# Retention followed by a squared-ReLU network: the first matrix product of ten groups in Strassen's form, with a table of priorities

## The chip, the cores and the metric

The kernel runs on one core of a Trainium2 chip. Its time is the device time of one execution in microseconds (us), as the median of several runs. A core has a matrix engine (TensorE; PE in the profile, with its weight loads as PEld), three engines for element-wise work (VectorE or DVE, ScalarE or ACT, GpSimd or POOL), an engine that here only issues transfers (SyncE or SP), and 16 DMA engines.

## The reference

Two stages. The first is a retention layer, attention without softmax: 8 batches, 8 heads, 576 positions, 64 numbers a head. The second takes its output, laid out as 4608 tokens of 512 numbers, through two matrix products with a squared ReLU between them.

```python
q, k, v: (8, 8, 576, 64) float32
scores = (1 / sqrt(64)) * q @ k^T
gamma[h] = 1 - 2 ** (-5 - h)
D[h, i, j] = gamma[h] ** (i - j) if i >= j else 0
a = (scores * D) @ v
x = a.transpose(0, 2, 1, 3).reshape(4608, 512)
h = x @ w_in                  # 512 x 2048
g = relu(h) ** 2
out = g @ w_out               # 2048 x 512, float32 result
```

## The kernel before

Matrix operands are float16, sums in PSUM and results float32. The tokens are cut into 36 **units** of 128: for each batch four chunks of 128 positions ("full" units) and, for the last 64 positions of two batches together, one "tail" unit. Two units make a **group** of 256 tokens; there are 18. Groups 0 to 3 are batches 0 and 1, groups 4 to 7 batches 2 and 3, group 8 the first two tail units, groups 9 to 12 and 13 to 16 the other four batches, group 17 the last two tail units.

What happens to a unit from 8 on: three loads (k, q, v; q as four transfers) are issued on SP's queue in `add_load` (L319, L316, for tails L322). GpSimd casts k and q to float16 into one tile `kq` (L394, L405) and multiplies v by a decay (L410). SP issues a DMA transpose of `kq` to `kqT` (L420). Units 0 to 7 come in pairs with wider loads and are transposed on TensorE (L461, tile psT).

What happens to a group: TensorE makes the scores (tile psc), the new states (psS) and the outputs (psO), all from small 64x64 matmuls recorded under L381. VectorE masks the scores (rT, L713), updates the states (Rm, stmp, and the decay to R, L487) and scales the outputs to `xT` (L772), which is x transposed: 128 partitions x 4 parts of the 512 numbers x 256 tokens. Scores and states of the next group are computed beside the outputs of this one.

Then the network, in `add_ff`. **First product**: 16 blocks of 128 of the 2048 columns; each is four matmuls of N=256 (one for each part of x; L896), two blocks to a PSUM tile `ph`. ScalarE takes the ReLU of a tile into `rl` (L904) and squares it into `gT` (L914); one tile in eight is squared on VectorE (L916). **Second product**, in `add_strassen`: for groups 1 to 17 it is already in Strassen's form (Winograd's variant). The product of 256 tokens x 2048 by 2048 x 512 is cut into 2x2 blocks; seven products of blocks (56 matmuls of N=256, L993, tile po) take the place of eight. For that VectorE makes four sums of blocks of g (`gS`, L966); four sums of w_out (`wT`, L848) were made once. ScalarE copies partial results out of PSUM (L1006, L1067), VectorE adds them into the output tile `o` (L1016), and SP stores it (L865, L870).

Engines and SP's queue each work strictly in order. The order is not written by hand: every piece of work is a task of class `Schedule` with an engine, a priority key, a planned duration, the tasks that it needs and the buffers that it takes. `emit` plays the tasks through in planned time; an engine that is free takes the ready task with the lowest key whose buffers are free, and instructions are emitted in that order. Keys before are formulas of the group number. The planner also slows VectorE's two-input float16 work (`soft` tasks) while GpSimd runs a long task. Buffers are counted in its dictionary: 5 for loads of each of k, q and v, 7 for `kq`, 7 for cast v, 6 for `kqT`, 3 for x, 4 for o, 8 banks of PSUM.

Of the kernel before, what the change touches and what calls it, by code (L numbers as in the profile page):

```python
# [9 lines left out]
FP32 = mybir.dt.float32  # L10
FP16 = mybir.dt.float16
ACTF = mybir.ActivationFunctionType
ALU = mybir.AluOpType


class Schedule:
# [9 lines left out]
    def add(self, eng, key, dur, fn, deps=(), acq=(), after=None, lag=0.0, soft=False):  # L26
        t = dict(soft=soft, eng=eng, key=key, dur=dur, fn=fn, acq=acq, n=len(self.tasks), users=[], free=[], lag=lag,
                 left=len(deps), ready=0.0, lat=self.LAT[eng] if after is None else after)
        for d in deps:
            d["users"].append(t)  # L30
        self.tasks.append(t)
        return t
# [11 lines left out]
    def emit(self):  # L44
        ready = {e: [] for e in self.LAT}
# [24 lines left out]
        while True:  # L70
            for e in ready:
                if busy[e]:
                    continue
                held = []
                while ready[e]:
                    item = heapq.heappop(ready[e])
                    t = item[2]
                    if all(self.count[r] >= t["acq"].count(r) for r in t["acq"]):
# [14 lines left out]
                    held.append(item)  # L93
                for item in held:
                    heapq.heappush(ready[e], item)
# [35 lines left out]
def kernel(  # L131
# [38 lines left out]
    ld = ctx.enter_context(tc.tile_pool(name="ld", bufs=5))  # L170
    stage = ctx.enter_context(tc.tile_pool(name="stage", bufs=4))
    cast = ctx.enter_context(tc.tile_pool(name="cast", bufs=7))
    work = ctx.enter_context(tc.tile_pool(name="work", bufs=4))
    o_pool = ctx.enter_context(tc.tile_pool(name="o", bufs=4))
    x_pool = ctx.enter_context(tc.tile_pool(name="x", bufs=3))
    st_pool = ctx.enter_context(tc.tile_pool(name="st", bufs=1))
    g_pool = ctx.enter_context(tc.tile_pool(name="g", bufs=3))
    u_pool = ctx.enter_context(tc.tile_pool(name="u", bufs=2))
    r_pool = ctx.enter_context(tc.tile_pool(name="r", bufs=3))
    ps_ff = ctx.enter_context(tc.tile_pool(name="ps_ff", bufs=8, space=bass.MemoryType.PSUM))  # L180
# [7 lines left out]
    wT = [const.tile([P, NF // 2, DM // 2], FP16, name=f"wT{i}") for i in range(4)]  # L188
    junk = wT[3][:, 0:2].rearrange("p f m -> p (f m)")
# [62 lines left out]
    for hp in range(NP):  # L252
# [19 lines left out]
    PAIRED = 8  # L272
    FIRST = ["k0", "q0", "v0", "k2", "q2", "v2", "w0", "w1", "w2", "w3", "w4", "w5", "w6", "w7", "k4", "q4", "v4", "k6", "q6", "v6"]
    sched = Schedule(dict(ff=8, prS=1, prO=1, g=3, ld=5, wst=4, kq=7, v16=7, rT=2, x=3, rl=3, o=4, p1=2, u2=2, u4=2,
                          R=5, Rm=2, kqT=6))
# [10 lines left out]
    def warm():  # L286
        if not warm_ps:
            warm_ps.append(ps_ff.tile([P, 512], FP32, name="warm", tag="ff"))
        nc.tensor.matmul(warm_ps[0], lhsT=junk[:, 0:P], rhs=junk, start=True, stop=True)  # L289
# [36 lines left out]
    def add_load_pair(name, u):  # L326
        n = "kqv".index(name)

        def fn():
            if name != "q":  # L330
                tile_of["stage", u] = stage.tile([P, 2, H, 2 * D], FP32, name="pair", tag="wst")
# [12 lines left out]
        loaded[name, u] = loaded[name, u + 1] = dma_task(0, 2.9 if not loaded else 1.41 if name == "q" else 1.81, fn, acq=("wst",) if name != "q" else (),  # L344
# [44 lines left out]
    def add_unit(u, base):  # L389
# [28 lines left out]
        def fx2():  # L418
            t = tile_of["kqT", u] = work.tile([P, 2 * NP, P], FP16, name="kqT", tag="kqT", bufs=6)
            nc.sync.dma_start_transpose(out=t, in_=tile_of["kq", u].rearrange("p x n -> p (x n)"))  # L420
        T["kqT", u] = [add("SP", -1, 2.60, fx2, deps=[ck, cq], acq=("kqT",), after=3.0, lag=LAG_T)]

    def add_unit_pair(u, base):
# [29 lines left out]
        sched.free("wst", xs["k"] + xs["q"])  # L453
        sched.free("wst", xs["v"])
        T["kqT", u], T["kqT", u + 1] = [], []
        for i, name in enumerate("kq"):
# [9 lines left out]
            for s in range(2):  # L466
                on_act = i == 0 or s == 0 or u > 0

                def fe(i=i, s=s, on_act=on_act):
                    if i == 0:  # L470
                        tile_of["kqT", u + s] = work.tile([P, 2 * NP, P], FP16, name="kqT", tag="kqT", bufs=6)
# [11 lines left out]
        T["kvx", u] = xs["k"] + xs["v"]  # L483

    def decay(out_, in_, n=2):
        shape = "p (s n d) -> p s n d"
        nc.vector.tensor_tensor(  # L487
# [6 lines left out]
    def add_ret_pair(g):  # L494
# [44 lines left out]
        def fr2(s):  # L539
            def f():  # L540
                if s == 0:
                    tile_of["R", g] = st_pool.tile([P, 2, NP * D], FP16, name="R", tag="R", bufs=5)
# [69 lines left out]
    def base_of(g):  # L612
        return (units_of(g)[0] - len(groups[g])) * L - EARLY
# [108 lines left out]
    def after_sums(g, t, key, res):  # L722
# [17 lines left out]
        def fr2():  # L740
            r = tile_of["R", g] = st_pool.tile([P, 2, NP * D], FP16, name="R", tag="R", bufs=5)
            decay(flat(r), flat(tile_of["tmp", g]))
# [4 lines left out]
        r2 = add("DVE", key + 0.3, 0.62, fr2, deps=[r1], acq=("R",), soft=True)  # L747
# [125 lines left out]
    T["ff2"] = []  # L873

# [3 lines left out]
    def add_ff(g):  # L878
        us = groups[g]
        n = len(us)  # L880
        base = min(us) * L

# [6 lines left out]
        for fb in range(NF // nf):  # L889
# [12 lines left out]
            def fr(fb=fb):  # L902
                t = tile_of["rl", g, fb] = r_pool.tile([P, nf, n * P], FP16, name="rl", tag="rl")
                nc.scalar.activation(out=t, in_=tile_of["ph", g, fb], func=ACTF.Relu)  # L904
# [3 lines left out]
            def fg(fb=fb, on_act=on_act):  # L908
                if fb == 0:
                    tile_of["g", g] = g_pool.tile([P, NF, n * P], FP16, name="gT", tag="gT")  # L910
                t = tile_of["g", g][:, nf * fb:nf * (fb + 1), :]
                rl = tile_of["rl", g, fb]
                if on_act:
                    nc.scalar.activation(out=t, in_=rl, func=ACTF.Square)  # L914
                else:
                    nc.vector.tensor_tensor(out=t, in0=rl, in1=rl, op=ALU.mult)  # L916
            r = add("ACT", place(4 * fb + 4) - HURRY * (g == 1 and fb == 7), 0.6, fr, deps=[f1[-1]], acq=("rl",))
            sched.free("ff", [r])
            sq.append(add("ACT" if on_act else "DVE", place(4 * fb + 6) - HURRY * (g == 1 and not on_act), 0.63 if on_act else 0.43, fg, deps=[r] + sq[:1],
                          acq=() if fb else ("g",), soft=not on_act))  # L920
            sched.free("rl", [sq[-1]])
        sched.free("x", [f1[-1]])
        base2 = base + NF * n
        if STRASSEN <= g:
            add_strassen(g, us, base2, sq)
# [26 lines left out]
    def add_strassen(g, us, base, sq):  # L952
# [7 lines left out]
        def add_sum(k, key, parts, in0, in1, op, deps, start=()):  # L960
# [171 lines left out]
```

## Time and profile before

| | |
|---|---|
| time, median of 3 runs (lowest to highest) | 289.2 us (288.98 to 289.39) |
| span of the profiled execution | 287.0 us |
| median less span | 2.2 us |
| mean granted TensorE clock | 0.998 |
| idle GpSimd time that ended with a landed k, q or v (units from 8 on) | 40.9, 32.3 and 24.8 us |
| DMA queue of SP | 114560 packets, 44.84 MB |

The span goes from the first to the last instruction of one profiled execution. The profile gives no time of its own for that execution, so the 2.2 us are what the median of the runs has over its span. A line of a group of instructions names source line, engine, operation, output and inputs, then the busy time, the mean of one in ns, and the idle time of the engine ahead of them with what ended it. A timeline line has start and duration in us and, in brackets, the idle time before. Durations of matmuls overlap, so their pace is read from the distance of their starts.

### The profile page before, as it was taken

How to read it: one execution, taken by the hardware profiler on the slowest of the kernel's cores; microseconds unless marked ns; L12 is line 12 of the kernel's file. 1: busy time of each engine (PE TensorE's matmuls, PEld its weight loads, DVE VectorE, ACT ScalarE, POOL GpSimd, SP SyncE). 2: the span in 40 equal slices, each digit the busy share in tenths (PEclk: the TensorE clock that was granted, in tenths of full speed). 3: DMA queues.
4: the chain of work that ended last, by engine and by line, in shares of the span. 5: the costliest groups of instructions: out<-in, count | busy, mean ns of one | idle time of the engine just before them, and what ended most of it. 6: DMA issues, size and time to landing. Idle time of an engine off the chain costs nothing.

```text
span 287.0 us, 10144 instructions
## 1 busy us (share of the span) xinstructions
PE 280.1 (98%) x4346; PEld 235.8 (82%) x4346; DVE 179.0 (62%) x340; ACT 189.1 (66%) x365; POOL 85.1 (30%) x123
## 2 busy tenths in 40 slices
PE   8899999999999999999999999999999999999994
PEld 3578768888888888888888888888888888888883
DVE  3783588666967557638376585867575567264632
ACT  5659984678476857759486767674857486728830
POOL 6550045333614342433424243342525000000000
PEclk9999999999999999999999999999999999999999
DMA  6999999979998897989999998979999220101004
GB/s 204 291 207 207 267 304 239 170 213 189 216 209 169 223 220 184 201 210 206 194 197 197 181 202 188 217 179 229 177 233 166 92 78 2 73 25 53 0 8 141
DMA packets 119149, 49.95 MB, mean 174 GB/s; under 512 B 94784, under 2 KB 113728, under 8 KB 119104
## 3 DMA queue, kind: packets, MB, share of 16 engines
q1 hardware_dynamic: 114560, 44.84, 69.4%
q0 software_dynamic: 4224, 4.19, 8.8%
q8 instruction: 34, 0.56, 0.8%
q10 hardware_dynamic: 320, 0.26, 0.4%
q14 instruction: 11, 0.09, 0.1%
HBM read 36.70 MB, written 9.44 MB: 161 GB/s over the span
## 4 chain that ended last, share of the span: by engine, by line
PE 94%; POOL 2%; issue 2%; DVE 0%; POOLq 0%; DVEq 0%
PE ph L896 44%; PE po L993 37%; PE psO L381 5%; PE po L936 2%; PE psS L381 2%; PE psc L381 2%; PE warm L289 1%; PE psT L461 1%; POOL mask L249 1%; POOL vx L439 0%; POOL w_in L355 0%; DVE o L1016 0%; POOL mask_full L241 0%; POOL mask_tail L241 0%; DVE p L1045 0%
## 5 line engine op out<-in xcount | busy, mean ns | idle before, releaser
L896 PE MATMUL ph<-xT,w_in 128*128 128x256 f16 x1152 | 136.9, 273 | 0.0
L896 PEld LDWEIGHTS <-w_in 128*128 128x128 f16 x1152 | 111.3, 98 | 14.2
L904 ACT ACTIVATE rl<-ph 128x512 f16<-128x512 f32 x144 | 84.3, 587 | 46.2 <-PE ph L896 44.7
L914 ACT ACTIVATE gT<-rl 128x512 f16<-128x512 f16 x118 | 74.4, 630 | 3.5
L993 PEld LDWEIGHTS <-gS 128*128 128x128 f16 x544 | 51.8, 98 | 6.6
L993 PE MATMUL po<-wT,gS 128*128 128x256 f16 x408 | 54.8, 273 | 0.0
L966 DVE TENSOR_TENSOR gS<-gT,gS 128x512 f16<-128x512 f16 (+1 forms) x51 | 31.1, 610 | 20.7 <-ACT gT L914 20.1
L993 PEld LDWEIGHTS <-gT 128*128 128x128 f16 x408 | 39.8, 98 | 4.9
L993 PE MATMUL po<-w_out,gT 128*128 128x256 f16 x272 | 36.7, 273 | 0.0
L410 POOL TENSOR_TENSOR v<-v,vdec_full 128x512 f16<-128x512 f32 x24 | 25.6, 1068 | 24.6 <-DMA v<-in_v_dram 22.5
L394 POOL CAST kq<-k 128x512 f16<-128x512 f32 x28 | 20.5, 733 | 41.7 <-DMA k<-in_k_dram 40.9
L966 DVE TENSOR_TENSOR gS<-gT 128x1024 f16<-128x1024 f16 x34 | 27.6, 813 | 6.4 <-ACT gT L914 6.3
L1006 ACT COPY u<-po 128x256 f32<-128x256 f32 x34 | 12.6, 369 | 25.1 <-PE po L993 25.0
L405 POOL CAST kq<-q 128x512 f16<-128x512 f32 x24 | 14.8, 618 | 32.5 <-DMA q<-in_q_dram 32.3
L1016 DVE TENSOR_TENSOR o<-po,u 128x256 f32<-128x256 f32 x33 | 13.9, 421 | 15.6 <-PE po L993 8.6
L772 DVE TENSOR_TENSOR xT<-psO,gam_full 128x512 f16<-128x512 f32 x28 | 18.0, 685 | 7.6 <-PE psO L381 7.4
L916 DVE TENSOR_TENSOR gT<-rl 128x512 f16<-128x512 f16 x26 | 11.6, 448 | 16.3 <-ACT rl L904 16.1
L713 DVE TENSOR_TENSOR rT<-psc,mask_full 128x512 f16<-128x512 f32 x24 | 15.5, 682 | 5.3 <-PE psc L381 5.2
L993 PE MATMUL po<-w_out,gS 128*128 128x256 f16 x136 | 17.8, 273 | 0.0
L993 PE MATMUL po<-wT,gT 128*128 128x256 f16 x136 | 17.6, 273 | 0.0
L1016 DVE TENSOR_TENSOR o<-po,p 128x256 f32<-128x256 f32 x18 | 7.6, 422 | 13.7 <-ACT u L1006 8.9
L487 DVE TENSOR_TENSOR R<-stmp,dec 128x512 f16<-128x512 f32 (+1 forms) x18 | 12.5, 694 | 0.5
(80 smaller groups left out, 219.3 us busy)
## 6 DMA issues: line engine op xcount, KB each, us to landing
out_dram<-o SPq DMA_DIRECT2D x32, 256.0 KB, 2.6
k<-in_k_dram SPq DMA_DIRECT2D x24, 256.0 KB, 4.5
q<-in_q_dram SPq DMA_DIRECT2D x96, 64.0 KB, 3.5
v<-in_v_dram SPq DMA_DIRECT2D x24, 256.0 KB, 3.9
pair<-in_k_dram SPq DMA_DIRECT2D x4, 512.0 KB, 7.1
pair<-in_q_dram SPq DMA_DIRECT2D x8, 256.0 KB, 5.9
pair<-in_v_dram SPq DMA_DIRECT2D x4, 512.0 KB, 5.5
w_in<-in_moe_w_in_dram POOLq DMA_DIRECT2D x4, 512.0 KB, 8.3
```

Source lines behind the costliest of these rows:

```text
L381: t = nc.tensor.matmul(out_, lhsT=lhsT, rhs=rhs, start=start, stop=True, skip_group_check=True, tile_position=(64 * row, 64 * col))
L394: op(out=out_.rearrange("p (n b a d) -> p n b a d", n=2, b=2, a=2), in_=in_.rearrange("p (a n b) d -> p n b a d", n=2, a=2))
L405: nc.gpsimd.tensor_copy(out=tile_of["kq", u][:, 1].rearrange("p (t a d) -> p a t d", t=4, a=2), in_=tile_of["q32", u].rearrange("p (a t) d ...
L410: nc.gpsimd.tensor_tensor(out=t, in0=tile_of["v32", u], in1=vdec[kind].rearrange("p (h o) -> p h o", o=1).to_broadcast([P, H, D]), op=ALU. ...
L713: tile_of["masking", g] = nc.vector.tensor_tensor(out=tile_of["rT", g][:, :, a], in0=tile_of["psc", g][a].rearrange("p (s n i) -> p s n i" ...
L772: nc.vector.tensor_tensor(out=tile_of["x", g].rearrange("p n (s e i) -> p e (n s) i", s=n, e=2)[:, c], in0=y.rearrange("p (o t r) -> p o r ...
L896: nc.tensor.matmul(tile_of["ph", g, fb][:, j, :], lhsT=w_in16[:, m, fi * P:(fi + 1) * P], rhs=tile_of["x", g][:, m, :], start=(m == 0), st ...
L904: nc.scalar.activation(out=t, in_=tile_of["ph", g, fb], func=ACTF.Relu)
L914: nc.scalar.activation(out=t, in_=rl, func=ACTF.Square)
L966: nc.vector.tensor_tensor(out=tile_of["S", g][:, k, sl], in0=in0(sl), in1=in1(sl), op=op)
L993: nc.tensor.matmul(tile_of["pb", g, bank], lhsT=left(i), rhs=right[:, i, :], start=(start and i == 0), stop=(i == HF - 1), skip_group_chec ...
L1016: nc.vector.tensor_tensor(out=o_tile(u)[:, half * HM:(half + 1) * HM], in0=bank(x), in1=tile_of[name, g], op=ALU.add)
```

## The change

Groups 5, 7 and 9 to 16 take the new function `add_ff1s` for the first product. x (512 numbers x 256 tokens) and w_in are cut into 2x2 blocks: 256 numbers by 128 tokens of x, 1024 columns by 256 numbers of w_in. Seven products follow for each half (j = 0, 1) of 512 columns: each is 8 matmuls of N=128 into a PSUM tile of 4 x 128. Four sums of x are made on GpSimd (three into a new tile `xS`, of which there is one; one in place in `xT`), four sums of w_in (`wS`, in eight VectorE instructions) once, into the tiles that had held the loads of units 0 and 4. Three partial results of each half are copied out of PSUM by ScalarE (p1q, u2q, u4q). Of the four blocks of a half, one gets its ReLU on ScalarE; three are made by a VectorE instruction that adds a PSUM tile and a copy and floors the sum at zero, straight into `gT`. ScalarE then squares in place, two blocks in one instruction.

Around it: in the other groups the ReLU goes straight into `gT` and is squared there (`rl` is gone). The decay of the states (R) of the groups from 4 on moves from VectorE to GpSimd. Buffers: loads 5 to 3, `kq` 7 to 6, cast v 7 to 6, o 4 to 3, wide loads and `gS` 4 to 3 with two fixed tiles beside them. The keys of nearly all of 1869 tasks come from a table (`PLACES`), and a task may not take a buffer that a task with a lower key on the same engine is waiting for.

```diff
+RESERVE = True
+PLACES = """
...
+""".split()
...
     def emit(self):
+        assert len(PLACES) == len(self.tasks)
+        for t, x in zip(self.tasks, PLACES):
+            if x != "-":
+                t["key"] = int(x)
...
-                    if all(self.count[r] >= t["acq"].count(r) for r in t["acq"]):
+                    if (t["inside"] or not kept.intersection(t["acq"])) and all(self.count[r] >= t["acq"].count(r) for r in t["acq"]):
...
+                    if RESERVE and t["key"] < 10 ** 5:
+                        kept.update(r for r in t["acq"] if self.count[r] < t["acq"].count(r))
...
+    H1, H2 = 2, 1
+    UF, OB, P1Q, WST = 2, 3, 2, 3
+    LD, KQ, V16, SB, G, UQ, KT, RB = 3, 6, 6, 0, 3, 2, 6, 5
...
+    FSET = (5, 7, 9, 10, 11, 12, 13, 14, 15, 16)
...
+    T_ENG = "POOL"
+    R_ENG = "POOL"
+    S4_ENG = "DVE"
...
-        r2 = add("DVE", key + 0.3, 0.62, fr2, deps=[r1], acq=("R",), soft=True)
+        r2 = add(R_ENG, key + 0.3, 0.62 if R_ENG == "DVE" else 1.07, fr2, deps=[r1], acq=("R",), soft=R_ENG == "DVE")
...
+    HK = NP // 2
+    wA = {(i, j): w_in16[:, HK * j:HK * j + HK, DFF // 2 * i:DFF // 2 * i + DFF // 2] for i in range(2) for j in range(2)}
...
+        s1 = add_wS(0, wA[1, 0], wA[1, 1], ALU.add, [])
+        s2 = add_wS(1, wS[0], wA[0, 0], ALU.subtract, [s1])
+        s3 = add_wS(2, wA[0, 0], wA[1, 0], ALU.subtract, [])
+        s4 = add_wS(3, wA[0, 1], wS[1], ALU.subtract, [s2])
...
+    def add_ff1s(g):
+
+        base = 2 * g * L - F1OFF
+        xs = [T["x", u] for u in groups[g]]
+        X = lambda i, s: (lambda: tile_of["x", g][:, HK * i:HK * i + HK, s * P:(s + 1) * P])
+        B11, B21, B12, B22 = X(0, 0), X(1, 0), X(0, 1), X(1, 1)
+        T1, T2, T4 = ((lambda i=i: tile_of["xs", g][:, HK * i:HK * i + HK]) for i in range(3))
+        T3 = B12
+        t = []
+        for i, (out_, in0, in1) in enumerate(((T1, B12, B11), (T3, B22, B12), (T2, B22, T1), (T4, B21, T2))):
+            def f(i=i, out_=out_, in0=in0, in1=in1):
+                if i == 0:
+                    tile_of["xs", g] = x_pool.tile([P, 3 * HK, P], FP16, name="xS", tag="xS", bufs=1)
+                (nc.vector if T_ENG == "DVE" else nc.gpsimd).tensor_tensor(out=out_(), in0=in0(), in1=in1(), op=ALU.subtract)
+            t.append(add(T_ENG, base - TKEY + i, 0.25 if T_ENG == "DVE" else 0.55, f, deps=xs + t, acq=() if i else ("xs",), soft=T_ENG == "DVE"))
...
+                for e in range(4):
+                    fi = 4 * j + e
+                    for m in range(HK):
+                        nc.tensor.matmul(out_[:, e], lhsT=left[:, m, fi * P:(fi + 1) * P], rhs=right()[:, m],
+                                         start=fresh and e == 0 and m == 0, stop=m == HK - 1, skip_group_check=True)
...
+        def relu_sum(s, h, j, x, name, key, deps, acq=()):
+            def f():
+                new_g()
+                nc.vector._custom_dve(TENSOR_ADD_SAT, out=g_at(s, h, j), in0=bank(j, x),
+                                      in1=tile_of[name, g, j].rearrange("p (e t) -> p e t", t=P), s0=3.4028234e38, s1=0.0)
+            return add("DVE", key - URGENT, 0.69, f, deps=deps, acq=acq)
...
+        for j in range(2):
+            at = lambda i, j=j: base + F1LEN * (JSTEP * j + i / 7 * (1 - JSTEP))
+            p1 = product(j, 1, "a", wA[0, 0], B11, xs, True, at(0))
...
+                c1 = copy_to("p1q", j, at(1.2), [p1])
+            p7 = product(j, 7, "c", wS[2], T3, [t[1], p1], True, at(1))
+            p6 = product(j, 6, "a", wS[1], T2, [t[2], c1, p7], False, at(2))
+            c2 = copy_to("u2q", j, at(3.2), [p6])
+            p2 = product(j, 2, "b", wA[0, 1], B21, xs + ([c1] if SEED1 else []) + [p6], not SEED1, at(3))
...
+                r11 = relu_sum(0, 0, j, "b", "p1q", at(4.5), [p2, c1], first)
...
+            p5 = product(j, 5, "a", wS[0], T1, [t[0], c2, p2], False, at(4))
+            c4 = copy_to("u4q", j, at(5.2), [p5])
+            r22 = relu_sum(1, 1, j, "c", "u4q", at(6), [p7, c4, r11])
...
+            p3 = product(j, 3, "a", wS[3], B22, [c4, p5], False, at(5))
+            r12 = relu_of(1, 0, j, "a", at(6.5), [p3, r11])
...
+            p4 = product(j, 4, "c", wA[1, 1], T4, [t[3], r22, p3], False, at(6))
+            r21 = relu_sum(0, 1, j, "c", "u2q", at(7), [p4, c2])
...
+            sq[0].append(square(0, j, at(8), [r11, r21]))
+            sq[1].append(square(1, j, at(8.5), [r12, r22]))
...
+        if strassen1(g):
+            sq = add_ff1s(g)
+            at = base + F2OFF
+            add_strassen(g, us, at, lambda s, i, h, parts: sq[s][h:h + 1] if parts == 2 else sq[s], lambda k: at + F2ST * k)
+            return
```

## The prediction

> **What bounds the kernel now.** I read the page first: busy shares, then the 40 slices.
>
> ```profile
> PE 280.1 (98%) x4346; PEld 235.8 (82%) x4346; DVE 179.0 (62%) x340; ACT 189.1 (66%) x365; POOL 85.1 (30%) x123
> PE   8899999999999999999999999999999999999994
> DMA  6999999979998897989999998979999220101004
> ```
>
> TensorE is busy all the time; the DMA engines are too, but only up to slice 31 (222 us). The chain of waits, in order of time, and TensorE's timeline give the pace of one matmul:
>
> ```profile
> 173.31 3.49 PE ph L896 x32
> ...
> 37.77 0.61 PE L461 MATMUL psT<-ident,kx 128*128 128x128 f16 x8
> 38.22 0.38 PE L936 MATMUL po<-w_out,gT 128*128 128x512 f16 x1
> ```
>
> 3.49/32 = 109 ns for N=256 with a new stationary tile each: an even pace, with no waiting in it to be won. The eight transposes are matmuls of N=128, each with its own stationary tile, and what follows starts 0.45 us after the first of them: 56 ns each. Third, windows of one group's length (busy time of PE, PEld, DVE, ACT, POOL; clock, DMA share, GB/s) and the timelines of SP's queue and of GpSimd where the loads end:
>
> ```profile
> 176.80:191.40 14.60, 14.60 (x251) 12.79 (x249) 10.90 (x17) 9.80 (x20) 5.65 (x8) 1.00 1.03 209
> 206.00:220.60 14.60, 14.60 (x250) 12.79 (x249) 9.64 (x17) 10.34 (x21) 6.17 (x7) 1.00 1.05 195
> 220.60:235.20 14.60, 14.60 (x250) 12.79 (x249) 8.65 (x16) 9.46 (x19) 1.04 (x1) 1.00 0.43 98
> ```
>
> ```profile
> 216.54 1.31 SPq L322 DMA_DIRECT2D v<-in_v_dram  x2
> 217.96 3.37 SPq L420 DMA_TRANSPOSE kqT<-kq  x2
> 221.43 1.44 SPq L865 DMA_DIRECT2D out_dram<-o  x2
> ```
>
> ```profile
> 219.45 0.61 POOL L394 CAST kq<-q 128x512 f16<-128x512 f32 x1 [0.17 <-DMA q<-in_q_dram]
> 220.80 1.04 POOL L410 TENSOR_TENSOR v<-v,vdec_tail 128x512 f16<-128x512 f32 x1 [0.74 <-DMA v<-in_v_dram]
> ```
>
> SP issues almost without a pause, and GpSimd sits waiting for data: the last v (unit 35) is cast only at 220.80. So there are two streams of nearly equal speed: TensorE at 14.6 us a group, and the loads at (220.09 - 53.21)/13 = 12.8 us a group, by the issue times of the last transpose of groups 17 and 4.
>
> **Own time.** The span is 287.0 and the median of the runs 289.2, so 2.2 us lie around the span. I sum in the span and add 2.2 at the end.
>
> **TensorE.** A direct group has 64 matmuls of N=256: 64 x 0.1092 = 6.99 us. A Strassen group has 7 products x 2 halves x 8 = 112 of N=128: 112 x 0.056 = 6.27. Saved: 0.72 a group, 7.2 in ten. Break-even pace: 6.99/112 = 62.4 ns. Bounds: 56 ns (the transposes) and 98 ns (the mean of one LDWEIGHTS, if weight loads could not overlap each other). I take 56, since in the transposes weight loads of 98 ns already follow each other at 56.
>
> A rule speaks against this change. The Trainium skill, TensorE: Matmul & The Clock Gate, Back-to-back issue gap, gives about 81 ns per matmul as the sustained pace of load-and-multiply pairs at N=128. By that, 112 matmuls take 9.07 us and ten groups lose 20.8 us. No run here shows more than 8 of N=128 in a row; the new blocks are of 8 or 16.
>
> **ScalarE.** New in a group: 6 copies and 2 relus of 128x512 (0.587, the row of rl) and 4 squares of 128x1024, each between 0.63 (the 128x512 square) and 1.26 (twice that): I take 1.1, 9.1 us together. Removed: 8 x 0.587 + 7 x 0.63 = 9.1. No change; 10 of 14 us stay. A copy (0.59) stands between products of one chain, which have two others (0.9 us) between them in the order: just covered, 0.1 to 0.3 us a product if it comes late.
>
> **VectorE.** New: 6 sums out of PSUM with a floor at zero, 128x512. Nearest row: xT, PSUM in, same size, 685 ns; bounds 0.42 (the o row, half the size) and 1.3. I take 0.685: 4.1. Removed: one square 0.45, one decay 0.75. Net +2.9 on about 9.3 a group: 12.2 of 14. The eight sums of weights (5.5 us at 0.69, the row of wT) are made once, before group 4. TensorE covers all this; uncovered it costs up to 2.9 a group.
>
> **GpSimd.** Four sums of 128x256: between 0.5 and 1.04 (half of and the whole v row); I take 0.55, as size decides in the o and xT rows. One decay of the v row's form, 1.04. Together +3.2 on 5 to 6 of 14 us: room enough by sums. gS reads SBUF twice and takes 684 ns by its median but 1537 at worst beside GpSimd, while o, from PSUM, stays at 421. So the new VectorE sums should not suffer, and I book 0.5 us a group for gS, hidden.
>
> One answer for the rest: relu writes straight into g (as many instructions of the same size); fewer o buffers and one fixed load tile cost nothing while stores go 5 us after the adds; the new priorities leave the first 15 us of TensorE's order nearly as it was.
>
> **The queues: where the gain goes.** SP keeps its instructions. Ahead of the last v load stand 26 transposes and 24 stores in both orders, so from a queue that always issues the last v lands when it did, 220.8. Three load buffers don't move that: a tile is cast soon after it lands. But GpSimd works in order, and the sums of x stand in its queue behind casts: group 5's behind k of unit 16 (cast at 93.84 before), 9's behind k of 24 (147.21), 11's behind k of 29 (179.24), 12's behind v of 31 (194.79), 14's behind v of 34 and 35 (220.80). The first product that reads such a sum (product 7) waits, and with it all that is queued on TensorE.
>
> Take group 14. Its sum is ready at 220.80 + 1.04 + 2 x 0.55 = 222.9. In the new order TensorE has, from that product on, 328 matmuls of N=128, 344 of N=256 and 240 small ones (9 ns each, by the 32 of psS from 212.62 to 212.90): 18.4 + 37.6 + 2.2 = 58.1 us. Before, the same situation: at 222.38 TensorE starts the scores of group 16 with 520 of N=256 and 272 small ones ahead, 59.2 us, and the span ends 64.6 later, 5.4 more than the sum (changes of block, the last adds and stores). New end: 222.9 + 58.1 + 5.4 = 286.4, with the 2.2 **288.6**. Without waiting that product would come at 216.0 (201.7 us of work ahead of it, and 14.2 us that TensorE was behind its sum there): a wait of 6.9 us that eats nearly all of the 7.2. The waits of the other groups' sums, 3 to 7 us, are the same one seen earlier; they don't add. Scores alone would wait 1.4 us at most (group 10).
>
> On top: unit 34's v needs the outputs of group 14 first (6 buffers for v instead of 7), so two casts may stand in a row, 0 to 1.0; late VectorE sums in the last 58 us, 0 to 1.5; sums ahead of casts that delay transposes, 0 to 1. I take 1.2: **289.8**.
>
> **Rivals.** *Forecast*: the loads gate, 288 to 291; 0.48.
> *TensorE stays the bound* (faster): 287.0 - 7.2 + 2.2 = 282.0 at best, 283.4 with the scores' wait, up to 288 where the loads come some us sooner. For it: DMA shares of 0.87 to 0.92 in some windows, two stores fewer ahead of the transposes of groups 10 to 12. Against: the order of GpSimd's queue, and pauses of only 5 us in SP's queue between 53 and 222. 0.28.
> *GpSimd's queue slows the loads* (slower): before, every second transpose is issued 0.03 us after its q cast ends (117.78 and 117.81, 143.20 and 143.23). Where sums and a decay (3.2 us) stand ahead of such a cast, SP's queue stops, and the loads behind it. Against: GpSimd idles 8 us of a group, mostly there. It decides once over 1.5 us of issue time is lost; five places of 0.7 to 1.3 us give 292 to 295. 0.20.
> *N=128 above 62.4 ns*: at 70 ns 7.6 x 1120 = 8.5 us lost, 298; at 98 ns 329. 0.04.
>
> **How the numbers follow.** No change is what three runs can hardly tell, 0.2% or 0.6 us: 288.6 to 289.8. Faster: 0.28, and 0.08 of the forecast's lower edge. Same: 0.18 of the forecast. Slower: its remaining 0.22, 0.20 and 0.04. The range leaves out some 0.1 below 285 and 0.08 above 294.
>
> **What will show it.** Right: ph at N=128 at 56 ns; waits of PE for GpSimd (xS, xT) of 1 to 5 us, first in group 5; the last v cast near 221 and product 7 of group 14 right after it; o still 421 ns. Wrong: the last v cast before 217 (gate gone, 285 or less) or after 224 (the slow rival); sums of x or the VectorE sums over 0.8 us; ph at N=128 over 62 ns.

## The result, and the profile after

The changed kernel takes 297.95 us (median of 4 runs, 295.56 to 299.88) against 289.2 us before in the same rounds (288.98 to 289.39): a ratio of 1.029, 95% interval 1.023 to 1.034. It is 8.7 us slower, where 289.8 was forecast and 294 was the upper end of the range. Its profiled execution took 297.86 us, with a span of 296.2 us and a mean granted clock (share of TensorE's full speed) of 0.988 (before: 0.998). Runs more than 1.5% above the fastest of the same kernel are left out of the times and ratios given here; with them the medians are 296.6 us for both_vector, 296.0 for move_t29, 292.4 for move_t29_vector and 287.3 for five_groups, which is how some of the expectations name them.

The page first, with the busy shares and the lines of the 40 slices (tenths of 7.4 us each) that answer to those of before, and the granted clock:

```profile
PE 277.8 (94%) x4826; PEld 240.1 (81%) x4826; DVE 210.2 (71%) x382; ACT 190.0 (64%) x339; POOL 127.1 (43%) x175
PE   8899999999996799999999999995999999999994
PEclk9999999999999799999999999997999999999999
DMA  7999997999999987999899896979898701010104
```

TensorE now has two holes (stretches in which it starts nothing, below also called stands), in slices 13 and 14 (93 to 98 us) and in slice 28 (199 to 203 us), and the granted clock drops right behind each. What TensorE waits for, from the waits of the whole span, is this (us in total, times, longest):

```profile
PE ph L1014 <- POOL xT L999: 5.3, 3, 4.7
PE psc L471 <- DMA kqT<-kq: 4.1, 1, 4.1
```

**The first hole** is group 5's sums of x. GpSimd's timeline (start, duration, what; in brackets the idle time before and what ended it):

```profile
93.88 1.04 POOL L500 TENSOR_TENSOR v<-v,vdec_full 128x512 f16<-128x512 f32 x1 [1.56 <-DMA v<-in_v_dram]
95.95 0.90 POOL L484 CAST kq<-k 128x512 f16<-128x512 f32 x1 [1.03 <-DMA k<-in_k_dram]
96.82 0.66 POOL L999 TENSOR_TENSOR xS<-xT 128x256 f16<-128x256 f16 x1
97.56 0.67 POOL L999 TENSOR_TENSOR xT<-xT 128x256 f16<-128x256 f16 x1
```

xT was ready at 91.0. The sums stand behind the casts of v of unit 15 and k of unit 16, and both casts wait for their loads; TensorE starts nothing from 93.4 to 98.3.

**The second hole** is the scores of group 14. SP's timeline and TensorE's:

```profile
184.94 1.27 SPq L510 DMA_TRANSPOSE kqT<-kq  x1
186.25 0.58 SPq L409 DMA_DIRECT2D k<-in_k_dram  x1
186.88 3.64 SPq L406 DMA_DIRECT2D q<-in_q_dram  x4
190.63 0.37 SPq L956 DMA_DIRECT2D out_dram<-o  x1
191.04 0.43 SPq L409 DMA_DIRECT2D v<-in_v_dram  x1
191.52 0.69 SPq L409 DMA_DIRECT2D k<-in_k_dram  x1
192.25 4.25 SPq L406 DMA_DIRECT2D q<-in_q_dram  x4
196.60 0.39 SPq L409 DMA_DIRECT2D v<-in_v_dram  x1
197.10 5.72 SPq L510 DMA_TRANSPOSE kqT<-kq  x3
```

```profile
198.90 0.30 PE L471 MATMUL psc<-kqT 64*64 64x64 f16 x12
203.31 0.32 PE L471 MATMUL psc<-kqT 64*64 64x64 f16 x16 [4.11 <-DMA kqT<-kq]
```

The transpose of unit 28 goes out at 184.94, that of unit 29 only at 197.10, with the loads of units 30 and 31 between them. Before, unit 29's went out at 180.97, ahead of those loads (SP's timeline before):

```profile
180.97 1.29 SPq L420 DMA_TRANSPOSE kqT<-kq  x1
...
182.93 1.55 SPq L319 DMA_DIRECT2D k<-in_k_dram  x1
```

The chain of waits shows the pace of the new product, and what the clock does to it behind the second hole:

```profile
153.69 1.34 PE ph L1014 x24
...
203.63 4.45 PE ph L1014 x48
```

1.34/24 = 56 ns as forecast; 4.45/48 = 93 ns at a clock that is half for most of it. And the loads no longer end at 221 us (GpSimd's timeline):

```profile
229.17 1.04 POOL L500 TENSOR_TENSOR v<-v,vdec_tail 128x512 f16<-128x512 f32 x1 [0.56 <-PE psO L471]
230.43 1.04 POOL L500 TENSOR_TENSOR v<-v,vdec_tail 128x512 f16<-128x512 f32 x1 [0.21 <-DMA v<-in_v_dram]
231.77 0.67 POOL L999 TENSOR_TENSOR xS<-xT 128x256 f16<-128x256 f16 x1 [0.30 <-PE ph L1014]
```

To tell TensorE's own work from its waits I split the time from its first to its last matmul. "Own pace" is, for each kind of matmul, their number times the median distance of two starts; the "rest" is all that is over: waits, changes of block, half clock. Each row is worked out from the trace of one execution; before and light_loads_before, 0.7 us apart in time, differ by 1.8 in the rest.

| kernel | time, us | own pace | rest | last v cast starts |
|---|---|---|---|---|
| before | 289.2 | 255.9 | 25.4 | 220.8 |
| after | 297.95 | 248.5 | 42.4 | 230.4 |
| light_loads_before | 289.9 | 255.7 | 27.2 | |
| light_loads | 289.1 | 248.7 | 32.8 | |
| light_no_weight_sums | 286.4 | 248.5 | 30.0 | |
| rest_only | 291.2 | 255.9 | 27.1 | 222.3 |
| five_groups | 287.0 | 252.0 | 26.8 | 223.2 |
| ten_groups_new_order | 296.05 | 248.5 | 41.2 | 228.5 |

The product does win its 7 us (255.9 - 248.5 = 7.4). The rest grows by 17.0, and 17.0 - 7.4 = 9.6 is the growth of the stretch; the span grew by 9.2. The question of the experiments is where the 17.0 come from.

### The profile page after: what moved, and what is told of

It is laid out like the page before. It is cut to its first block, busy times and chain, and to the rows that moved or that the text cites. A ratio compares the mean times of both kernels' runs of the same rounds, so it can differ in the third digit from the quotient of the medians.

```text
span 296.2 us, 11160 instructions
## 1 busy us (share of the span) xinstructions
PE 277.8 (94%) x4826; PEld 240.1 (81%) x4826; DVE 210.2 (71%) x382; ACT 190.0 (64%) x339; POOL 127.1 (43%) x175
## 3 DMA queue, kind: packets, MB, share of 16 engines
q1 hardware_dynamic: 114560, 44.84, 71.0%
## 4 chain that ended last, share of the span: by engine, by line
PE 71%; DMA 11%; DVE 5%; SPq 5%; POOL 4%; ACT 1%; issue 1%; DVEq 0%; POOLq 0%; ACTq 0%
PE po L1218 31%; PE ph L1014 20%; PE ph L1123 12%; DMA w_out<-in_moe_w_out_dram 5%; SPq L406 3%; PE psO L471 3%; DMA pair_c<-in_k_dram 2%; DMA kqT<-kq 2%; PE warm L379 2%; DVE pair_c L976 2%; DMA k<-in_k_dram 2%; PE psc L471 2%; PE psS L471 1%; DVE rx L605 1%; POOL xS L999 1%
## 5 line engine op out<-in xcount | busy, mean ns | idle before, releaser
L1123 PE MATMUL ph<-xT,w_in 128*128 128x256 f16 x512 | 62.0, 273 | 1.3 <-DVE rx L605 0.7
L1123 PEld LDWEIGHTS <-w_in 128*128 128x128 f16 x512 | 49.2, 98 | 8.9 <-DMA w_in<-in_moe_w_in_dram 1.2
L1132 ACT ACTIVATE gT<-ph 128x512 f16<-128x512 f32 x64 | 37.3, 590 | 15.1 <-PE ph L1123 14.5
L1014 PEld LDWEIGHTS <-pair_c 128*128 128x128 f16 x640 | 41.1, 100 | 7.1 <-issue 5.6
L1055 ACT ACTIVATE gT<-gT 128x1024 f16<-128x1024 f16 x40 | 42.2, 1060 | 3.2 <-DVE gT L1043 2.6
L1014 PEld LDWEIGHTS <-w_in 128*128 128x128 f16 x480 | 31.8, 101 | 0.9
L1139 ACT ACTIVATE gT<-gT 128x512 f16<-128x512 f16 x52 | 31.8, 628 | 0.8
L1014 PE MATMUL ph<-xT,pair_c 128*128 128x128 f16 x320 | 24.8, 223 | 5.4 <-POOL xT L999 5.3
L1014 PE MATMUL ph<-xT,w_in 128*128 128x128 f16 x320 | 25.2, 226 | 0.0
L1014 PE MATMUL ph<-xS,pair_c 128*128 128x128 f16 x320 | 25.1, 224 | 0.0
L1024 ACT COPY u2q<-ph 128x512 f32<-128x512 f32 x20 | 11.7, 585 | 19.1 <-PE ph L1014 19.0
```

Of the source, the lines that this page charges most:

```text
L1014: nc.tensor.matmul(out_[:, e], lhsT=left[:, m, fi * P:(fi + 1) * P], rhs=right()[:, m], start=fresh and e == 0 and m == 0, stop=m == HK - ...
L1055: nc.scalar.activation(out=t, in_=t, func=ACTF.Square)
L1123: nc.tensor.matmul(tile_of["ph", g, fb][:, j, :], lhsT=w_in16[:, m, fi * P:(fi + 1) * P], rhs=tile_of["x", g][:, m, :], start=(m == 0), st ...
L1132: nc.scalar.activation(out=tile_of["g", g][:, nf * fb:nf * (fb + 1), :], in_=tile_of["ph", g, fb], func=ACTF.Relu)
```

## The experiments

Theories: **A**, the in-order queue of GpSimd (sums and decays between casts) ties TensorE to the loads. **B**, the load stream sets the end whoever makes the sums, slowed by the smaller buffers (without the buffers it is the "stream theory" of later expectations). **Stalls**, single places of the order cost what they cost, and go when moved. All ratios are against the kernel before in the same rounds.

**Sums of x, then decays too, on VectorE, at the same places of the order.**

```diff
-                (nc.vector if T_ENG == "DVE" else nc.gpsimd).tensor_tensor(out=out_(), in0=in0(), ...
+                nc.vector.tensor_tensor(out=out_(), in0=in0(), ...
...both_vector only:
-            decay(flat(r), flat(tile_of["tmp", g]), eng=nc.gpsimd if R_ENG == "POOL" else nc.vector)
+            decay(flat(r), flat(tile_of["tmp", g]), eng=nc.vector)
```

> The changed kernel with one edit: the four sums of x of each of the ten groups (40 instructions of 128x256) are issued on VectorE instead of GpSimd, at the same place of the written order; every other engine keeps its order. Time of the changed kernel: 297.9 us. Theory A (GpSimd's in-order queue ties TensorE to the loads: TensorE stands at 94.0 to 98.9 because group 5's sums are queued behind a cast that waits for a load, and 4 us at a granted clock near 0.55 follow, 4.9 + 1.8 = 6.7 us): that stand disappears, and q casts no longer stand behind sums that wait for xT, so the last v cast comes before 226; 289 to 292 us. Theory B (the load stream alone sets the end, whoever makes the sums; it is slower because of the smaller buffers): TensorE only waits later and longer, the last v cast stays at 229 to 231, 295 to 298 us. Theory C (VectorE's extra 4 x 0.4 us a group hurts): over 298 us.

> As sums_vector, and the state decays of the single units go back to VectorE too (12 instructions of 128x512): GpSimd does only what it did before the change. Theory A: GpSimd then never waits for VectorE's stmp (11.5 us in the changed kernel), so 1 to 3 us below sums_vector, 287 to 290 us, last v cast 220 to 224. Theory B (the stream alone, smaller buffers): still 295 to 298, last v cast at 229 to 231. If only the sums matter: equal to sums_vector within 1 us.

297.5 us (1.024, 1.017 to 1.031) and 296.5 (1.019, 1.009 to 1.028). The hole at 94 us is gone in both, as A said, but the second is there (3.7 us, from 197.4 and 197.5), the last v is cast at 228.5, and the time hardly moves. In its plain form A falls: with GpSimd doing just what it did before, the last v is still 8 us late. GpSimd's waits in both_vector show a tie to TensorE that is left; the two longest of it:

```profile
POOL v L500 <- PE ph L1014: 5.1, 3, 2.2
POOL v L500 <- PE psO L471: 3.8, 2, 3.1
```

Now casts of v wait for TensorE, 13.0 us in all between 75 and 232 us (3.8 before). By the kernel's order what such a cast needs from TensorE is a free buffer, one whose v has been read out.

**Small buffers alone, and the change without its table.**

```diff
-    ld = ctx.enter_context(tc.tile_pool(name="ld", bufs=5))
+    ld = ctx.enter_context(tc.tile_pool(name="ld", bufs=3))      # kq and v16: 7 to 6
```

> The kernel before with only its buffer counts changed: loads 5 to 3, casts of k and q 7 to 6, of v 7 to 6 (the order is planned anew with them). Kernel before: 289.2 us, last v cast at 220.8. Theory A (buffers don't matter): 289 to 291 us, last v cast at 220 to 222. Theory B (the smaller buffers slow the load stream): last v cast at 227 to 231; TensorE has some 60 us of work behind it, so 294 to 298 us.

289.6 us, 1.000 (0.998 to 1.003), last v cast at 222.5. In the kernel before the smaller buffers cost nothing: B's second half falls there.

```diff
-        assert len(PLACES) == len(self.tasks)
-        for t, x in zip(self.tasks, PLACES):
-            if x != "-":
-                t["key"] = int(x)
```

> The changed kernel without its table of priorities: all priorities are those that the formulas give; GpSimd keeps sums and decays, buffers stay small. If the table is what makes the sums wait (its places were tuned to another timing): 290 to 296 us. If the table is a help and the queue of GpSimd is the cause (theory A): 298 to 306 us, with waits of TensorE for xS and xT again. Theory B: within 2 us of 297.9.

306.1 us (1.056, 1.050 to 1.063): the table as a whole is a help, worth 8 us.

**Single places moved.** Two edits of the written order: M5, group 5's sums ahead of the casts of v of unit 15 and k of unit 16; M29, the q cast of unit 29 ahead of its v cast, and its transpose ahead of the loads of unit 31.

```diff
+        for n, where, anchor in ((287, 'before', 288), (289, 'before', 131)):    # M29
+            t = self.tasks[n]
+            order.remove(t)
+            order.insert(order.index(self.tasks[anchor]) + (where == "after"), t)
```

> The changed kernel (297.9 us) with one place of GpSimd's written order changed: the four sums of x of group 5 stand ahead of the casts of v of unit 15 and k of unit 16 instead of behind them. Nothing else moves. Stalls theory (TensorE's time is its work plus single stands that an order causes; the stand at 94 to 99 costs 4.9 us and 1.7 us more in the 3.4 us at half clock behind it): the stand and that stretch of half clock go; 291 to 293 us if nothing takes their place. Stream theory (the end is set by the load stream, last v cast at 230): TensorE only stands longer at 199, for unit 29's transpose, which is issued at 197.1 as before; 296 to 298 us.

> The changed kernel with another place changed: on GpSimd the cast of q of unit 29 stands ahead of the cast of v of the same unit and of a decay, and in SP's queue its transpose stands ahead of the loads of unit 31 instead of behind them (it was issued at 197.1 us; before the change at 181.0). Stalls theory: the stand of 4.3 us before the scores of group 14 (199.0 to 203.3) and the half clock behind it (1.7) go; 291 to 293 us. Stream theory: the last v is cast at 229 to 231 all the same, TensorE waits later; 296 to 298 us.

> Both moves together. Stalls theory: both stands and both stretches of half clock go, 4.9 + 1.7 + 4.3 + 1.7 = 12.6 us: 285 to 288 us, the change then being a gain. Stream theory: 294 us or more, since 58 to 60 us of TensorE's work and the tail stand behind the last v cast at 229 or later. If new stands appear (scores of groups 15 to 17 waiting for transposes, sums of group 14): in between, 289 to 293 us.

> both_vector (sums of x and decays on VectorE; 296.6 us) with the move of unit 29's cast and transpose. Its one large stand, 3.7 us before the scores of group 14, and the 3.4 us at half clock behind it go: stalls theory 290 to 292 us; stream theory 294 to 297 us. Beside move_both it shows which engine is the better place for the sums once that order is mended.

295.6 us with M5, 295.9 with M29, 295.8 with both, 291.8 with M29 and both_vector (1.018, 1.022, 1.025, 1.009; intervals 1.012 to 1.025, 1.020 to 1.025, 1.018 to 1.032, 1.006 to 1.012). Each move takes its hole away or most of it, and a new one opens. With M5, in the execution that was profiled (292.3 us, the shortest of its runs), the second hole is gone too: the longest stand is 2.7 us at 181.1, for sums of x, and the last v is cast at 224.9. With M29, GpSimd and TensorE show this (source lines are 4 further down there):

```profile
196.50 0.61 POOL L499 CAST kq<-q 128x512 f16<-128x512 f32 x1
198.20 2.04 POOL L504 TENSOR_TENSOR v<-v,vdec_full 128x512 f16<-128x512 f32 x2 [1.08 <-DMA v<-in_v_dram]
200.20 0.67 POOL L1003 TENSOR_TENSOR xS<-xT 128x256 f16<-128x256 f16 x1
200.94 0.67 POOL L1003 TENSOR_TENSOR xT<-xT 128x256 f16<-128x256 f16 x1
```

```profile
196.68 0.42 PE L475 MATMUL psc<-kqT 64*64 64x64 f16 x28
201.66 1.01 PE L1018 MATMUL ph<-xT,pair_c 128*128 128x128 f16 x8 [4.55 <-POOL xT L1003]
```

Instead of group 14's scores it is now group 12's sums that come late, behind the casts of v of units 30 and 31: the very kind of wait that the prediction had at group 5. The stalls theory falls in this form: of the four, only move_t29_vector (291.8) lies in the window that it gave (290 to 292).

**Mixed engines for the sums.**

```diff
-                (nc.vector if T_ENG == "DVE" else nc.gpsimd).tensor_tensor(...
+                (nc.vector if g in (5, 11, 12, 14) else nc.gpsimd).tensor_tensor(...    # mixed, with M29
```

> move_t29 (296.0 us) with the sums of x of groups 5, 11, 12 and 14 on VectorE (0.28 us each there, 0.67 on GpSimd), the other six groups' on GpSimd. In move_t29 TensorE stands 1.6 us for group 5's sums, 0.6 for group 11's, 4.75 for group 12's (queued behind unit 31's v cast), with 1.7 us of half clock behind the last; in move_both 3.6 us for group 14's. Stalls theory: these go, 286 to 290 us. Stream theory: new stands take their place, 293 us or more.

> move_t29 with all sums of x on VectorE and the decays left on GpSimd: between move_t29 (296.0) and move_t29_vector (292.4, decays on VectorE too). If what is left there is VectorE being late (stands of TensorE for o and gS of 2.4 and 1.5 us at 155 and 169), taking 12 decays of 0.75 us off VectorE helps: 288 to 291 us. If decays in GpSimd's queue hold up casts (GpSimd waits 11.5 us for stmp in the changed kernel): 293 to 296 us.

295.8 us (1.019, 1.014 to 1.025) and 294.7 (1.017, 1.012 to 1.022). In mixed a stand of 3.2 us for sums of x opens at 211.9; in t29_sums_vector no stand is over 1.6 us, but ten of 0.6 to 1.6 us add up, and the last v is at 227.6. Its time is in the second window: with the decays on GpSimd the kernel is slower than with them on VectorE (move_t29_vector, 291.8), though the two intervals just touch.

**Loads taken out.** For units 8 to 35 only k is loaded, and the casts of q and v read its tile; what remains is the change with a third of its load stream.

```diff
+                if name != "k":
+                    tile_of[name + "32", u] = tile_of["k32", u]
+                    return
                 x = ld.tile([P, H, D], FP32, name=f"{name}32", tag=f"{name}32")
```

> The changed kernel with two thirds of the loads of units 8 to 35 left out: only k is loaded, and the casts of q and v read k's tile; all instructions of GpSimd, VectorE, ScalarE and TensorE stay, and the transposes and stores too. If TensorE's stands (13.4 us in all of over 0.25 us, and two stretches of half clock) come from the load stream, through casts, sums queued behind casts and transposes: they nearly go, and the 7.2 us that N=128 saves show: 289.2 - 7.2 = 282 at best, 282 to 286 us. If they come from the work itself (sums on GpSimd, VectorE 71% busy, the copies on ScalarE, N=128): 290 us or more.

> The kernel before (289.2 us) with the same loads left out; the control for light_loads. TensorE was at work 98% of its span, so at most what it waits early on is to be had: 287.5 to 289.5 us. Had the kernel before been held by its loads anywhere, it would fall by more, and the gain of the product in light_loads must be counted from here.

The control stays at 289.9 us (1.000, 0.999 to 1.002): before the change these loads did not hold the kernel. The changed kernel falls from 297.95 to 289.1 (0.998, 0.997 to 1.000). All its large stands are gone; the longest left after 44 us is 1.1 us. So 8.8 us hang on the load stream; by what way, this run does not tell. But I had expected 282 to 286, and that missed too: against the control TensorE's own pace is 7.0 shorter and the rest 5.6 longer.

**And the sums of weights taken out.** The products use parts of w_in as they are.

```diff
-                    nc.vector.tensor_tensor(out=wS[i][:, :, sl], in0=in0[:, :, sl], in1=in1[:, :, sl], op=op)
+                    pass
```

> light_loads (289.1 us) with the eight sums of weights left out as well (products 3, 5, 6 and 7 take parts of w_in as they are); the order of all else is the same. In light_loads TensorE's own pace is 7.0 us shorter than in the kernel before with the same loads left out, but its waits are 5.7 us longer, 2.7 of them between 20 and 70 us, where VectorE works without a pause at the sums of weights. If these eight (0.7 to 1.4 us each) are what it waits for there: 286 to 287 us. If they are hidden, as the prediction had it: 288.8 to 289.5 us, and the lost gain sits in the Strassen groups themselves.

286.4 us (0.989, 0.984 to 0.993), 2.7 less. The window from 44 to 62 us of both (length, then busy time of PE, PEld, DVE, ACT, POOL), first light_loads, then light_no_weight_sums:

```profile
44.00:62.00 18.00, 16.06 (x278) 13.06 (x280) 17.29 (x28) 9.40 (x19) 10.47 (x11) 1.00 0.81 156
```

```profile
44.00:62.00 18.00, 17.82 (x377) 14.52 (x376) 13.19 (x24) 11.88 (x23) 9.34 (x12) 1.00 0.87 149
```

With the sums VectorE is busy 17.29 of 18 us, and TensorE only 16.06; without them 13.19 and 17.82. There VectorE is the bound, and 1.8 us of TensorE are lost in this window alone. With all loads the same window shows it too: VectorE 16.91 and TensorE 16.58 us in the changed kernel, 12.20 and 17.82 before.

**What stands beside the ten groups.** No group in `FSET`; the formulas' keys.

```diff
-    FSET = (5, 7, 9, 10, 11, 12, 13, 14, 15, 16)
+    FSET = ()
```

> The change without its first part: no group takes its first product by Strassen (the table, which belongs to the ten groups, is replaced by the formulas' priorities); the smaller buffers, the decays on GpSimd, relu written into g and the eight sums of weights (made, not used) stay. Kernel before: 289.2. If the loss of 8.7 us comes from the ten groups and their order: 289 to 291.5 us, last v cast near 221. If it comes from what stands beside them: 294 us or more.

291.2 us (1.006, 1.003 to 1.009): 1.7 us of loss come from what stands beside the ten groups: weight sums, decays, buffers and relu in place, in the formulas' order.

**Does GpSimd's slower sum matter without loads to wait for?** light_loads with the edits of both_vector.

> light_loads (289.1 us) with the sums of x and the decays on VectorE at the same places of the order. If TensorE's remaining waits of about 0.7 us in some groups (99, 122 us) come from sums that take 4 x 0.67 us on GpSimd: 287 to 288.5 us. If VectorE, then at some 80%, is late instead: 289 to 292 us.

288.3 us (0.997, 0.995 to 0.999) against 289.1 (0.998, 0.997 to 1.000): 0.8 us by the medians at most, and the intervals overlap, so a gain is not shown.

**Fewer groups and an order with slack.** Sums and decays on VectorE, weight sums spread over groups 5 to 8, and a table searched anew: priorities were kept where the kernel's planner finished early both with its own durations and with loads and vector work that come later.

```diff
-    FSET = (5, 7, 9, 10, 11, 12, 13, 14, 15, 16)
+    FSET = (9, 11, 13, 15, 16)          # four_groups: (9, 11, 13, 15)
-    T_ENG = "POOL"
-    R_ENG = "POOL"
+    T_ENG = "DVE"
+    R_ENG = "DVE"
...
-                              deps=[d[h] for d in deps] + T["kvx", 4] + T["qx", 4] + sum((wcast[x] for x in range(4)), []), soft=True))
+                              deps=[d[h] for d in deps] + T["kvx", 4] + T["qx", 4] + sum((wcast[x] for x in range(4)), []) + [T["x", 2 * (5 + (2 * i + h) // 2)]], soft=True))
```

> A version meant to beat both: the first product by Strassen in groups 9, 11, 13, 15 and 16 alone, sums of x and decays on VectorE, the sums of weights spread over groups 5 to 8, and a table of priorities searched anew with slack for late loads. 5 x 0.72 = 3.6 us to be had, less 1 to 2 us of waits. If order and slack decide (stalls theory): 286 to 288.5 us, no stand of TensorE over 2 us, granted clock 1.0 throughout. If every Strassen group costs more in waits than it saves: 290 to 294 us.

> The same with groups 9, 11, 13 and 15 alone and a table of its own: 4 x 0.72 = 2.9 us to be had, less 1 to 2 us of waits. Stalls theory: 286.5 to 289 us; otherwise 290 us or more.

> The changed kernel (ten groups, sums of x and decays on GpSimd, weight sums before group 5) with nothing but the table's numbers changed: it was searched anew for slack against late loads, in the same way as for five_groups, but starting from the change's own table. Stalls theory: an order with slack loses less, 289 to 294 us; what the weight sums (2.7 us) and the sums on GpSimd cost stays, so it does not beat 287.3. If ten groups leave no order with slack, because loads at 12.8 us a group come hardly faster than TensorE then works (13.9): 294 to 300 us, with stands of over 2.6 us again.

five_groups takes 287.0 us, 0.991 of the kernel before (0.988 to 0.994): it beats both. Its page:

```profile
PE 276.1 (97%) x4586; PEld 236.7 (83%) x4586; DVE 201.4 (71%) x389; ACT 190.8 (67%) x354; POOL 86.8 (30%) x123
PE   7799999999999999999999999999999999999994
PEclk9999999999999999999999999999999999999999
```

No hole, no drop of the clock. VectorE is as busy as in the changed kernel (71%), so its share alone was not what hurt. four_groups is level with before (288.5; 0.997, 0.994 to 1.001), for all its promise of 2.9 us. ten_groups_new_order is not better than the change (296.05; 1.022, 1.016 to 1.027): no stand over 2.2 us, but eight of 0.7 to 2.2, six of them for sums of x on GpSimd. Within ten groups, and with the sums on GpSimd, the search found no order with slack; that none exists is not shown. Which of the four differences of five_groups does how much was not tried apart.

## Why the prediction was wrong

**Right.** *TensorE*: ph at N=128 runs at 56.0 ns by the median of its 1120 matmuls, 7.2 us were forecast and 7.4 are there. The Trainium skill's rule (TensorE: Matmul & The Clock Gate, Back-to-back issue gap) of some 81 ns is not what this trace shows; by it 20.8 us would have been lost here and not won. *ScalarE*: 189.1 before, 190.0 after; the square of 1024 took 1060 ns (1.1 taken). *VectorE's prices*: the sums out of PSUM 685 to 688 ns (0.685 taken), o still 421. *The first wait*: PE for GpSimd in group 5, 1 to 5 us said, 4.7 measured. *Three load buffers alone*: no effect, as said.

**A little off.** The sums of x took 0.67 to 0.71 on GpSimd where 0.55 was taken (bounds 0.5 to 1.04); on VectorE, in both_vector, 0.28 by the median. The Trainium skill (GPSIMD Engine Reference, Engine selection) says about twice as slow for two inputs; here it is 2.4 times. By light_both_vector this and the decays cost 0.8 us at most. The 2.2 us around the span were 1.7 to 2.0 in the four runs of the changed kernel.

**Wrong, and this is the failed step**: "from a queue that always issues the last v lands when it did, 220.8". The prediction took the load stream of before as given and let TensorE wait for it, once. The last v was cast at 230.43, 9.6 us later, and that is nearly all that the sum missed (a span of 286.4, measured 296.2). From product 7 of group 14 to the end it had 58.1 + 5.4 = 63.5 us, and 63.0 were measured, from this line of TensorE's timeline on:

```profile
233.24 0.61 PE L1014 MATMUL ph<-xT,pair_c 128*128 128x128 f16 x8 [0.22 <-POOL xT L999]
```

But this product waited 0.2 us for its sum, not 6.9: TensorE had lost its time before, at the two holes.

Why the last v comes late is shown only in part. My reading is a loop. SP's queue also holds transposes that wait for casts, and GpSimd's queue holds work that waits for TensorE and VectorE. In the changed kernel SP waits 9.5 us for GpSimd's xS, xT and R (4.2, 2.9 and 2.4), which were not in that queue before, and GpSimd waits for what VectorE makes of TensorE's results. These waits of GpSimd, from 75 to 232 us, while there are loads to cast:

```profile
POOL R L578 <- DVE stmp L829: 11.2, 3, 6.0
POOL xS L999 <- DVE xT L863: 4.7, 2, 3.2
```

So the loads would wait for TensorE while TensorE waits for the loads, and a delay on either side would come back to it; move_g5, where the second hole went with the first, fits this. Where TensorE does not stand (before, before_small_buffers, rest_only, five_groups) the last v starts at 220.8 to 223.2; in the kernels of ten groups with all their loads at 224.9 or later.

The record also has figures against the loop as the whole cause. The 9.5 us mostly take the place of waits for casts: SP's waits for GpSimd are 31.8 us in all (53 to 232 us), and 30.3 before (53 to 222). From 53 us to the issue of the last v load (at 226.9, before at 217.2) pauses of over 0.1 us and semaphore instructions take SP 8.4 us, before 5.0; most of the rest lies in issues that take longer, the 96 of q 63.0 us against 56.5. In both_vector SP stands 5.4 us, hardly more than before, and the last v load still goes out at 225.0. A rival is slower transfer: the same 114560 packets of SP's queue take 71.0% of 296.2 us and not, as before, 69.4% of 287.0 (210 against 199 us of the engines). They take 199 to 203 us where the last v load goes out by 222.3 (the four kernels above, formula_order, move_g5 and mixed), and 210 to 214 in sums_vector, both_vector, move_t29, t29_sums_vector and ten_groups_new_order, where it goes out between 222.9 and 225.0; four_groups lies between (207, at 220.4). Whether slow packets delay the loads or crowded loads slow the packets no run tells. What is shown is that the forecast's end of the stream was wrong, by 9.6 us, and that with two thirds of the loads left out 8.8 us go, and both holes; the way from the ten groups to the late stream stays open.

**Not as forecast**: "The waits of the other groups' sums, 3 to 7 us, are the same one seen earlier; they don't add." Two stands came behind different loads, 4.9 us at 93 and 4.3 us at 199, the second for scores, where 1.4 us at most were forecast, and none came at group 14. Whether the two add to the end, or only took early what the late stream would have cost there, these runs do not tell. And the prediction counted the instructions ahead of the *last* v in SP's queue, 26 transposes in both orders, but not whether each transpose kept its place: unit 29's moved behind six loads.

**Wrong**: "TensorE covers all this", of VectorE's new work. The weight sums cost 2.7 us with the loads taken out (light_loads against light_no_weight_sums): they were put where VectorE then has hardly a gap from 44 to 62 us, and took 7.3 us in the changed kernel (5.5 forecast). The share of a whole group (12.2 of 14 us) hid one crowded stretch.

**Missing**: the clock. Behind both holes it is 0.5 for 3.41 us, half of which, 1.7 us, is lost each time.

The rival "GpSimd's queue slows the loads" (292 to 295, 0.20) was nearest in kind: SP's queue did stand 3.4 us longer, over the 1.5 that it named, and the last v came after 224, its sign. But it had neither the longer issues nor the weight sums. In all: 7.4 us won, 8.8 lost on what hangs on the loads (297.95 - 289.1) and 2.7 on the weight sums. If these add up, 8.7 + 7.4 - 8.8 - 2.7 = 4.6 remain; against the control it is 3.7, as 289.9 less 7.2 of own pace is 282.7 and light_no_weight_sums took 286.4. Up to 0.8 of it may be the sums and decays on GpSimd; the rest, such as stands of under 1.2 us in the groups, was not taken apart further.

## What to carry to other kernels

When two streams run at nearly one pace, don't take the slower one's end as given while you change the other: look for each wait that leads back from one to the other (here a likely way, not a proven one), and give the late end a price of its own. Check the place of each single transfer, not only the number of those ahead of the last one, and the busy share of the one stretch into which one-time work is put, not that of the average group. Taking out the suspected resource (here two thirds of the loads) with a control told in two runs what eight moves of single pieces could not: how much of the loss hangs on it.

## What the hardware showed that I had not expected

A short stand of TensorE can cost more than its length. After the first 20 us the profiles of all runs show twelve stands of over 2.6 us (distance of two matmul starts). Eleven were followed by a stretch at a granted clock of 0.5, of 3.41 us in seven cases and 6.83 in four; the one of 3.57 us in move_both was not. Of fifteen stands of 1.4 to 2.6 us two were. The Trainium skill (TensorE: Matmul & The Clock Gate, Part 1) has the rule: activity is judged in windows of about 3.4 us, and an idle window halves the clock. The length agrees; but here 2.69 us of standing (move_g5), and in two cases 1.8 and 2.1, were enough, while 3.57 were not.

The changed kernel's times also spread more: 4.3 us between its shortest and longest run, 0.4 us before in the same rounds, and the runs' clocks go from 0.977 (299.88 us) to 0.991 (295.56 us).
